# Scaling x by V's bound, turning it by halves of heads, and a new order of issue in a kernel of bucketed attention and a gated MoE

## The chip, the cores and the metric

One core of one Trainium2 chip runs the whole program. The metric is the device time of one execution in microseconds (us); lower is better. Engines are named as the profile names them: PE (TensorE, matmuls; PEld is its weight loads), DVE (VectorE), ACT (ScalarE), POOL (GpSimd), SP (SyncE, which issues the DMAs).

## What is computed

```python
# B, H, S, D = 4, 8, 768, 64; six hash bits; 3072 tokens, d_model 512, d_ff 1536
q_bits = einsum('bhsd,dk->bhsk', q, proj) > 0      # k_bits likewise
mask   = q_bucket[:, :, :, None] == k_bucket[:, :, None, :]
scores = where(mask, q @ k.T / sqrt(D), -1e9);  scores -= max(scores)
attn   = exp(scores);  attn /= sum(attn) + 1e-9
x      = (attn @ v).transpose(0, 2, 1, 3).reshape(B * S, H * D)
out    = ((x @ w_a) * (x @ w_b)) @ w_out
```

All inputs and the output are f32.

## The kernel before

**Precision.** PE works on f16. An f32 operand is scaled by a power of two and split into a high and a low f16 half, and a product is three matmuls (high by high, high by low, low by high). So each operand needs a scale: the largest magnitude per partition, `mx`, is turned by a small matmul (`ps_k`, `ps_v`, `ps_w`, L460 and L590), reduced (`al`, L466), and made into a power of two by three or four tiny DVE instructions (`scale_of`, L472 to L480; `w_scale`, L596 to L605).

**Attention.** The work is cut by batch (4), chunk of 256 tokens (3 a batch) and half of the heads (2): 24 units. `kprep` and `qprep` split K and Q (`split`, L883 on ACT or L887 on DVE for the high half, L904 for the low one), and turn them with token and feature axes exchanged (`turn`: for the first pair of K heads and the first Q by PE, `t_k` and `t_q`, with the copies L863 and L865; for all others by a DMA transpose, L844). `buckets` multiplies by proj's two halves (L816), adds the two columns of each hash bit on DVE (L825) and marks the operand with plus or minus a large number for each bit (L829), so that tokens of unequal buckets get a score far below all others. `vprep` scales V per pair of heads (`vsc`, four `ps_v` a batch; `veps`, L780) and splits it (`vh` L790, `vl` L802). `qtile` makes the scores `s` (L1053), their maximum `mx` on DVE (L1067), `width` and `bias` (L1076, L1083, L1089; `qsig` of `widths`, L995), the exponentials `e` on ACT (L1099), two f16 parts `a` (casts L1110 to L1112, low parts L1122 on POOL or L1126 on DVE), a DMA transpose `at` (L1132) and the product `av` (L1141). The first two units work in f32 with transposes `et`/`ec` by PE (`by_pe`, L1020 to L1034).

**End of a unit.** `su_end` (L1149) makes `r` (guarded sum, L1166 or L1171, and reciprocal L1179) and `x` = `av` times `r` (L1184), then the sums of |x| per token (L1195). When both halves of a chunk are there, `norm` makes a power of two per token (L1210 to L1219: 4 tiny DVE instructions for each of 2 token tiles), x is scaled by it and split (`xz`, L1237 and L1248), and each token tile is turned by one DMA transpose into `xT` (L1260). In the first and the last chunk PE turns x instead (`px`, L1283), after POOL has scaled it (L1269), and ACT and DVE write the two halves (L1295, L1298).

**MoE.** For each chunk `moe` runs twelve groups `f`: 24 matmuls `ab` (L1346), an ACT pass `a` (L1360), the product `g` on DVE (L1368), its high half (L1376 or L1380) and low half (POOL, L1388), six matmuls `o` (L1398). At the end `osc` undoes the scales per token (L1417) and `ob` is evicted (L1428, L1434, L1443) and stored (L1452). Weights are loaded (L529) and split in the first batch, beside the attention of that batch (`load_group`, `w_group`, `wo_group`, L564 to L658).

**Order.** Every operation is entered in a plan with an engine and a cost, and then issued in the order of a searched list `ORDER` (L104). A number names an operation; one above 10000 takes its first alternative engine, above 20000 its second; a negative number issues that many matmuls `warm` (L1502), which multiply an identity and are read by nobody:

```python
            if x < 0:
                fill(-x)
                continue
            which, at = divmod(x, 10000)
            o = self.ops[at]
            (o.alt[which - 1][2] if which else o.fn)()
```

Each engine then runs its own instructions strictly in that order.

Of the kernel before, what the change touches and what calls it, by code (L numbers as in the profile page):

```python
# [1540 lines left out]
```

## Time and profile before

| | |
|---|---|
| three runs | 891.77, 890.8, 888.18 us; median 890.8 |
| the profiled execution | own time 892.62 us, span 890.8 us |
| busy share of the span | PE 97%, DVE 73%, ACT 61%, POOL 48% |
| instructions | PE 9258 matmuls, DVE 1575, ACT 1043, POOL 373 |
| granted TensorE clock, mean | 0.996 of full speed |

Share of the span is an average over stages that differ. Reading starts with windows of time (which engine is full where), then goes to the chain of waits within the window that matters, and then to single groups of instructions.

### The profile page before, as it was taken

The page shows a single profiled execution, that of the slowest core. Times are in us where ns is not written, and L with a number is a line of the kernel's source. Part 1 is how long each engine was busy: PE and PEld are TensorE (multiplying, and loading weights), DVE is VectorE, ACT ScalarE, POOL GpSimd, SP SyncE. Part 2 cuts the span into 40 slices and gives each one's busy share as a digit, 9 for nine tenths or more (in the row PEclk, how much of TensorE's full clock was granted, in tenths as well). Part 3 has the DMA queues.
Part 4 walks back from the last instruction along what each step waited for, and adds up shares of the span by engine and source line. Part 5 has one row for each costly group of instructions (what it writes and reads, how often), then busy time and mean ns, then how long its engine had stood idle before and what let it go on. Part 6 is the DMA issues. An engine that isn't in the chain of part 4 may idle for free.

```text
span 890.8 us, 23135 instructions
## 1 busy us (share of the span) xinstructions
PE 866.6 (97%) x9258; PEld 661.0 (74%) x9258; DVE 650.1 (73%) x1575; ACT 542.6 (61%) x1043; POOL 425.0 (48%) x373
## 2 busy tenths in 40 slices
PE   6899999999999999999999999999999999999998
PEld 5678777777777777777777777777777777777775
DVE  6998999988877778878865676786888866663211
ACT  6998899976565685665644367536766555442212
POOL 2568788656345464563332455443455254342111
PEclk9998999999999999999999999999999999999999
DMA  9877799999999989998957598997999876645000
GB/s 325 314 157 225 133 259 190 191 188 191 169 193 204 162 145 182 199 182 176 191 103 135 84 194 142 174 201 140 174 172 168 142 139 113 117 87 92 1 24 25
DMA packets 416988, 142.61 MB, mean 160 GB/s; under 512 B 388592, under 2 KB 409200, under 8 KB 416880
## 3 DMA queue, kind: packets, MB, share of 16 engines
q1 hardware_dynamic: 416880, 141.14, 81.2%
q8 instruction: 72, 1.18, 0.5%
q14 instruction: 36, 0.29, 0.1%
HBM read 37.82 MB, written 6.29 MB: 50 GB/s over the span
## 4 chain that ended last, share of the span: by engine, by line
PE 82%; DVE 7%; DMA 6%; ACT 1%; issue 1%; POOL 1%; SPq 0%; ACTq 0%; DVEq 0%; POOLq 0%
PE ab L1346 39%; PE o L1398 20%; PE s L1053 12%; PE av L1141 9%; DMA at<-a 3%; DVE mx L1067 2%; DMA qTA_q<-marked 1%; DMA rk_k<-in_k_dram 1%; DVE wmx L634 1%; DMA raw_w<-in_moe_w_b_dram 1%; DVE wab L573 1%; PE av L1034 1%; POOL a L1122 1%; PE b_k L816 0%; DVE vl L802 0%
## 5 line engine op out<-in xcount | busy, mean ns | idle before, releaser
L1346 PE MATMUL ab<-xT,wab 128*128 128x256 f16 x3456 | 408.8, 273 | 0.9 <-DVE g L1368 0.9
L1346 PEld LDWEIGHTS <-wab 128*128 128x128 f16 x3456 | 332.8, 98 | 59.3 <-issue 2.4
L1388 POOL TENSOR_TENSOR g<-g,g 128x256 f16<-128x256 f32 x144 | 109.3, 759 | 291.0 <-ACT g L1376 155.7
L1122 POOL TENSOR_TENSOR a<-e,a 128x768 f16<-128x768 f32 x121 | 205.6, 1705 | 85.0 <-ACT a L1111 38.7
L1099 ACT ACTIVATE e<-s,bias,width 128x768 f32<-128x768 f32 x192 | 189.5, 987 | 56.7 <-DVE bias L1089 42.2
L1398 PE MATMUL o<-wo,g 128*128 128x512 f16 x864 | 207.6, 379 | 0.7 <-DVE ob L1434 0.7
L1067 DVE TENSOR_REDUCE mx<-s 128x1 f32<-128x768 f32 x192 | 182.0, 949 | 33.3 <-PE s L1053 32.4
L1368 DVE SCALAR_TENSOR_TENSOR g<-ab,wlow,a 128x256 f32<-128x256 f32 x132 | 63.6, 482 | 136.5 <-ACT a L1360 120.7
L1360 ACT ACTIVATE a<-ab,wcut 128x256 f32<-128x256 f32 x144 | 67.8, 471 | 151.1 <-PE ab L1346 149.3
L1398 PEld LDWEIGHTS <-g 128*128 128x128 f16 x864 | 81.8, 98 | 78.5 <-issue 0.8
L1141 PEld LDWEIGHTS <-at 128*128 128x128 f16 x3168 | 111.3, 98 | 18.0 <-DMA at<-a 4.6
L1141 PE MATMUL av<-vh,at 128*128 128x64 f16 x2112 | 114.8, 193 | 2.4 <-DMA at<-a 2.2
L1053 PE MATMUL s<-kTA_k,qTA_q 128*128 128x384 f16 x384 | 94.6, 328 | 3.7 <-ACT e L1099 1.8
L1053 PE MATMUL s<-kTB_k,qTB_q 128*128 128x384 f16 x384 | 94.2, 327 | 0.0
L1111 ACT CAST a<-e 128x768 f16<-128x768 f32 x85 | 70.3, 828 | 5.5 <-DMA at<-a 2.7
L1083 ACT ACTIVATE bias<-mx,width 128x1 f32<-128x1 f32 x98 | 28.6, 293 | 70.8 <-DVE width L1076 70.6
L1126 DVE TENSOR_TENSOR a<-e,a 128x768 f16<-128x768 f32 x55 | 57.5, 1049 | 8.2 <-ACT a L1111 6.0
L1112 POOL CAST a<-e 128x768 f16<-128x768 f32 x48 | 40.2, 838 | 43.4 <-ACT e L1099 23.2
L1141 PE MATMUL av<-vl,at 128*128 128x64 f16 x1056 | 59.7, 193 | 0.0
L1053 PEld LDWEIGHTS <-qTB_q 128*128 128x128 f16 x384 | 37.7, 98 | 25.3 <-issue 0.7
L1376 ACT CAST g<-g 128x256 f16<-128x256 f32 x78 | 31.2, 400 | 30.9 <-DVE g L1368 25.3
L1053 PEld LDWEIGHTS <-qTA_q 128*128 128x128 f16 x384 | 33.9, 100 | 18.6 <-issue 5.5
(156 smaller groups left out, 877.6 us busy)
## 6 DMA issues: line engine op xcount, KB each, us to landing
rk_k<-in_k_dram SPq DMA_DIRECT2D x16, 384.0 KB, 4.2
vr<-in_v_dram SPq DMA_DIRECT2D x16, 384.0 KB, 4.1
rq_q<-in_q_dram SPq DMA_DIRECT2D x12, 512.0 KB, 4.8
raw_w<-in_moe_w_b_dram SPq DMA_DIRECT2D x12, 512.0 KB, 7.4
raw_w<-in_moe_w_a_dram SPq DMA_DIRECT2D x12, 512.0 KB, 7.3
raw_wo<-in_moe_w_out_dram SPq DMA_DIRECT2D x12, 512.0 KB, 5.6
out_dram<-ob SPq DMA_DIRECT2D x24, 256.0 KB, 3.0
at<-a SPq DMA_TRANSPOSE x176, 4.1
```

What stands on the lines that cost most here:

```text
L1053: nc.tensor.matmul(ps.t[:, jj, :HALF], lhsT=x.t[:, uq, :], rhs=y.t[:, h * NT + jj * 3 : h * NT + jj * 3 + 3, :].rearrange("p t x -> p (t x)"),
L1067: lambda: nc.vector.tensor_reduce(out=mx.t[:, u : u + 1], in_=halves(ps.t), axis=AX.XY, op=ALU.max, negate=True),
L1099: lambda: nc.scalar.activation(flat2(e.t), halves(ps.t), AF.Exp, bias=bias.t[:, u : u + 1], scale=width.t[:, u : u + 1], accum_out=sm.t[:, ...
L1111: ("ACT", 0.725, lambda: nc.scalar.copy(out=a2.t[:, 0], in_=e.t), False),
L1122: lambda: nc.gpsimd.tensor_tensor(out=a2.t[:, 1], in0=e.t, in1=a2.t[:, 0], op=ALU.subtract),
L1126: lambda: nc.vector.tensor_tensor(out=a2.t[:, 1], in0=e.t, in1=a2.t[:, 0], op=ALU.subtract), True,
L1141: nc.tensor.matmul(av.t[:, u, :], lhsT=at.t[:, a + kt, :], rhs=w.t[:, h, kt, :], start=i == 0, stop=i == 3 * NT - 1,)
L1346: nc.tensor.matmul(pl.t[:, m, :CH], lhsT=wt(m, wi, cc, f), rhs=xt.t[:, :, xi * NC + cc, :], start=i == 0, stop=i == 3 * NC - 1,)
L1360: lambda a=a, pl=pl, gr=gr: nc.scalar.activation(a.t, pl.t[:, 0, :CH], AF.Copy, scale=wcut[:, gr : gr + 1]),
L1368: lambda a=a, g32=g32, pl=pl, cut=cut: nc.vector.scalar_tensor_tensor(out=g32.t, in0=pl.t[:, 1, :CH], scalar=cut, in1=a.t, op0=ALU.mult, o ...
L1388: lambda g=g, g32=g32: nc.gpsimd.tensor_tensor(out=g[1].t, in0=g32.t, in1=g[0].t, op=ALU.subtract),
L1398: nc.tensor.matmul(po.t[:, u, :], lhsT=g[gi].t[:, us], rhs=wo[f // 2].t[:, f % 2, wi * DM : (wi + 1) * DM], start=f % per_q == 0 and i == ...
```

## The change

- x is no longer normalised per token. `x_scale` makes one factor per batch from V's scales (`xinv`, `xrel`), which enters through `r`; the sums of |x|, `norm` and POOL's scaling of x are gone; `osc` is one number per chunk. In the first two units `r` is made on DVE, elsewhere on ACT or DVE.
- x is turned by halves of heads: each unit writes its own `z` (high half by ACT, DVE or POOL, low half by DVE or POOL) and issues one DMA transpose of 8 blocks, as many in all as before; in the first and last chunk one `px` of 4 blocks per unit.
- In the first batch V has one scale (`vscale_all`): four magnitudes, one `ps_v`. That matmul stands on PE right ahead of the first `t_q`, and all four V loads stand ahead of the first weights. `vh` and `vl` share a tile `vv`; `veps` is gone.
- The two columns of each hash bit are summed by PE (two accumulating matmuls) for K of the first batch and for the first Q: 64 tiny matmuls more, 5 reductions on DVE fewer.
- `widths` is one instruction in place of two (24 in place of 48 in all); the weights' `wcut` and `wone` are made for two groups at once.
- The very last `o` is issued per token tile, and the last `ob` is evicted in two halves, by ACT and by DVE.
- POOL is a new alternative for the high halves of K, Q and V. The list uses it 6, 7 and 9 times; ACT makes 4 high halves of K (before 11), 3 of Q (11) and 6 of V (14).
- `ORDER` is new. It has 112 `warm` matmuls in place of 192. In both lists all of them stand ahead of the first `ab`; ahead of the 17th score tile stood 160 of 192 and now stand 111 of 112. In all ACT has 725 instructions in place of 821, DVE 1416 in place of 1577, POOL 402 in place of 378.

```diff
-                out=sums.t[:, :, half], in_=x.t.rearrange("p (j t h) d -> p t j (h d)", j=2, t=TPC), axis=AX.XY,
-                op=ALU.add, apply_absolute_value=True,
...
-        op("DVE", 1.32, norm, key, r=[(sums, 0), (sums, 1)], w=[sc, sq])
...
+        def guarded_whole():
+            nc.vector.tensor_scalar(
+                out=r.t, in0=sm.t, scalar1=1e-9, scalar2=xinv[:, 0, 1:2], op0=ALU.add, op1=ALU.mult
+            )
...
+            z = buf("z", [P, 2, 2 * TPC, P], F16, f"z_{n}", 1)
...
+                lambda: nc.sync.dma_start_transpose(
+                    out=xt.t[:, half].rearrange("p i u x -> p (i u) x"), in_=z.t.rearrange("p i u x -> p (i u x)")
+                ),
+                key, r=[(z, "hi"), (z, "lo")], w=[(xt, half)], svc=2.2 * 8 / 12,
...
+    def vscale_all(keys, tag):
+        mx = buf("sc_mx4", [P, NPAIR + 1], F32, "mx_v", 1)
+        for hp in range(NPAIR):
+            magnitude(
+                v32[0, hp], vjunk(0, hp), lambda hp=hp: mx.t[:, hp + 1 : hp + 2], keys[hp], [(mx, hp), (vv[0, hp], "lo")]
+            )
+        op(
+            "DVE", 0.13,
+            lambda: nc.vector.tensor_reduce(out=mx.t[:, 0:1], in_=mx.t[:, 1:], axis=AX.X, op=ALU.max),
+            keys[-1], r=[(mx, hp) for hp in range(NPAIR)], w=[mx],
+        )
+        scale_of(mx, vsc[:, 0:1], xinv[:, 0, 1:2], ("v1", 0), "v", keys[-1], tag=tag)
...
             for u in range(n):
+                if summed:
+                    for i in range(2):
+                        nc.tensor.matmul(
+                            ps.t[:, 1, u * NBITS : (u + 1) * NBITS], lhsT=tB.t[:, u, :], rhs=pw[:, :, i],
+                            start=i == 0, stop=i == 1,
+                        )
+                    continue
...
+            ), (
+                "POOL", 0.1 + 0.065 * n,
+                lambda: nc.gpsimd.tensor_scalar(
+                    out=part(B, hi_at), in0=x, scalar1=sc.t, scalar2=1.0, op0=ALU.mult, op1=ALU.mult
+                ),
+                False,
...
+            for us_ in [[u] for u in range(TPC)] if alone and f == NF - 1 else [range(TPC)]:
...
+                if alone and u == TPC - 1:
+                    hs = [slice(0, DM // 2), slice(DM // 2, DM)]
...
-    6, 5, 7, 13, 4, 2, 1, 0, 53, 41, 61, 281, 277, 276, 10014, 8, 280, 9, 3, 258, 10, 15, -10, 11, 254, 257, 16,
+    4, 5, 6, 7, 13, 0, 41, 2, 1, 53, 56, 54, 55, 266, 14, 265, 3, 261, 15, -9, 262, 16, 240, 17, 42, 239, 10018, 243,
```

**ACT, ahead of the first scores.** Of before, and then of the change, from the copy of `kTA` on; `nB_k_1,mx_k_1` is the magnitude of the second K load, `qTA` the first Q that the first scores need, `raw_w` weights. The line numbers are those of each file.

```order
L863 COPY kTA_k_0_321<-t_k_0_ACT 128x1536
L550 ACTIVATE raw_w_0_125<-raw_w_0_125,wsc_335 128x1024
L550 ACTIVATE raw_w_1_123<-raw_w_1_123,wsc_335 128x1024
L751 ACTIVATE nB_k_1_400,mx_k_1_401<-rk_k_1_81 128x12x64
L863 COPY qTA_q_0_408<-t_q_0_ACT 128x2048
L790 ACTIVATE vh_0_164<-vr_0_118,vsc 128x768
```

```order
L928 COPY kTA_k_0_323<-t_k_0_ACT 128x1536
L557 ACTIVATE raw_w_0_134<-raw_w_0_134 128x1024
L549 ACTIVATE raw_w_1_128<-raw_w_1_128,wsc_373 128x1024
L549 ACTIVATE raw_w_0_134<-raw_w_0_134,wsc_373 128x1024
L928 COPY qTA_q_0_411<-t_q_0_ACT 128x2048
L758 ACTIVATE nB_k_1_421,mx_k_1_422<-rk_k_1_82 128x12x64
```

The magnitude of K's second load stood ahead of the copy of `qTA` and now stands behind it; one more pass over weights stands ahead.

**SP, ahead of the second Q's transpose.** Of before and of the change; `qTA_q_1` is the marked Q of the second chunk, `raw_w` and `rq` are loads of 0.5 MB.

```order
L844 DMA_TRANSPOSE qTB_q_1_935<-nB_q_1_741 128x16x128
L734 DMA vr_3_957<-in_v_dram 128x2x384
L529 DMA raw_w_0_973<-in_moe_w_b_dram 128x1024 x2
L529 DMA raw_w_1_986<-in_moe_w_a_dram 128x1024
L949 DMA rq_q_0_89<-in_q_dram 128x8x128
L529 DMA raw_w_1_1013<-in_moe_w_b_dram 128x1024
L529 DMA raw_w_0_1024<-in_moe_w_a_dram 128x1024 x2
L529 DMA raw_w_1_1013<-in_moe_w_b_dram 128x1024
L844 DMA_TRANSPOSE qTA_q_1_1065<-marked 128x16x128
```

```order
L909 DMA_TRANSPOSE qTB_q_1_880<-nB_q_1_789 128x16x128
L909 DMA_TRANSPOSE kTA_k_3_928<-marked 128x12x128
L1022 DMA rq_q_2_87<-in_q_dram 128x8x128
L528 DMA raw_w_1_951<-in_moe_w_b_dram 128x1024
L528 DMA raw_w_0_849<-in_moe_w_b_dram 128x1024
L1022 DMA rq_q_0_90<-in_q_dram 128x8x128
L528 DMA raw_w_1_1022<-in_moe_w_a_dram 128x1024
L528 DMA raw_w_1_951<-in_moe_w_b_dram 128x1024
L909 DMA_TRANSPOSE qTA_q_1_1040<-marked 128x16x128
```

Nine loads stood between the last transpose and this one; now six stand there.

**POOL, first third of the first batch.** Of before and of the change; `marked` is the operand that gets the bits' marks, `vv` V's halves, `wab` weights.

```order
L895 COPY marked<-nB_k_0_128 128x12x64
L564 TENSOR_SCALAR raw_w_1_123<-raw_w_1_123 128x1024
L564 TENSOR_SCALAR raw_w_0_159<-raw_w_0_159 128x1024
L895 COPY marked<-nB_k_1_400 128x12x64
L564 TENSOR_SCALAR raw_w_1_137<-raw_w_1_137 128x1024
L564 TENSOR_SCALAR raw_w_1_411<-raw_w_1_411 128x1024
```

```order
L958 TENSOR_SCALAR nB_q_0_158<-rq_q_0_83,qsc_q_0_223 128x16x64
L563 TENSOR_SCALAR raw_w_1_128<-raw_w_1_128 128x1024
L830 TENSOR_SCALAR vv_3_187<-vr_3_122,vsc 128x12x64
L966 COPY marked<-nB_q_0_158 128x16x64
L830 TENSOR_SCALAR vv_1_225<-vr_1_124,vsc 128x12x64
L830 TENSOR_SCALAR vv_0_179<-vr_0_120,vsc 128x12x64
L563 TENSOR_SCALAR raw_w_0_151<-raw_w_0_151 128x1024
L563 TENSOR_SCALAR raw_w_1_164<-raw_w_1_164 128x1024
L958 TENSOR_SCALAR nB_k_1_421<-rk_k_1_82,ks_k_1_451 128x12x64
L830 TENSOR_SCALAR vv_2_232<-vr_2_126,vsc 128x12x64
```

The high halves of the first Q, of V and of two K pairs, which ACT made, are now among POOL's instructions.

## Rows read from the trace of the kernel before

**Rows 1.** The page: busy us by engine; granted clock, tenths, in 40 slices.

```profile
PE 866.6 (97%) x9258; PEld 661.0 (74%) x9258; DVE 650.1 (73%) x1575; ACT 542.6 (61%) x1043; POOL 425.0 (48%) x373
...
PEclk9998999999999999999999999999999999999999
```

**Rows 2.** Windows: length; busy PE, PEld, DVE, ACT, POOL; clock, DMA share, GB/s.

```profile
0.00:25.00 25.00, 16.12 (x163) 12.32 (x164) 16.83 (x50) 17.88 (x21) 5.39 (x13) 1.00 0.92 334
25.00:110.00 85.00, 78.01 (x713) 64.20 (x712) 78.18 (x200) 76.44 (x127) 61.23 (x42) 0.96 0.80 201
110.00:150.00 40.00, 37.95 (x433) 28.32 (x431) 37.61 (x91) 37.80 (x61) 31.96 (x22) 1.00 1.13 238
80.00:90.00 10.00, 8.58 (x44) 7.16 (x43) 6.04 (x14) 5.61 (x10) 5.86 (x4) 0.66 0.15 48
150.00:300.00 150.00, 148.82 (x1702) 113.19 (x1701) 125.47 (x323) 102.64 (x201) 83.16 (x71) 1.00 1.01 184
```

**Rows 3.** PE by line: the filling matmuls, and the bits of K.

```profile
L1502 PE MATMUL warm<-ident 128*128 128x256 f16 x192 | 27.6, 289 | 0.0
...
L816 PE MATMUL b_k<-pjk,kTB_k 128*128 128x12 f16 x192 | 7.2, 168 | 0.3 <-DVE kTA_k L865 0.3
```

**Rows 4.** Chain of waits, 20 to 110 us: shares; start us, us, what.

```profile
by line: DVE mx L1067 14.7%; DMA qTA_q<-marked 13.7%; DMA rk_k<-in_k_dram 12.0%; DVE wmx L634 7.9%; DVE wab L573 6.4%; issue 5.7%; PE av L1034 5.6%; POOL a L1122 5.3%; DMA at<-a 4.3%; PE s L1053 4.2%; PE et L1020 2.8%; DVE wo_y L573 2.5%; P
...
21.97 0.94 ACT nB_k L751 x2
...
22.91 1.76 ACT qTA_q L863
...
69.30 12.36 DMA qTA_q<-marked
```

**Rows 5.** PE timeline around 82 us: start us, us, what [idle].

```profile
78.83 1.45 PE L1034 MATMUL av<-vr,ec 128*128 128x64 f32 x12
...
81.70 0.50 PE L1053 MATMUL s<-kTA_k,qTA_q 128*128 128x384 f16 x2 [1.42 <-DMA qTA_q<-marked]
...
83.53 2.66 PE L1034 MATMUL av<-vr,ec 128*128 128x64 f32 x12
```

**Rows 6.** DVE by line, 0 to 150 us: xcount | busy, mean ns.

```profile
L1195 DVE TENSOR_REDUCE sums<-x 128x2 f32<-128x512 f32 x2 | 1.3, 670 | 0.0
...
L825 DVE TENSOR_REDUCE b_k<-b_k 128x72 f32<-128x144 f32 x4 | 1.2, 308 | 0.0
...
L995 DVE TENSOR_SCALAR qsig_q<-kinv,qmx_q 128x1 f32<-128x1 f32 x10 | 1.6, 205 | 0.0
...
L466 DVE TENSOR_REDUCE al_v<-ps_v 128x1 f32<-128x128 f32 x4 | 1.1, 282 | 0.6 <-PE ps_v L460 0.6
...
L605 DVE TENSOR_SCALAR wcut<-wcut 128x1 int32<-128x1 int32 x6 | 0.9, 154 | 0.2
```

**Rows 7.** DVE by line, whole span: the low parts `a`.

```profile
L1126 DVE TENSOR_TENSOR a<-e,a 128x768 f16<-128x768 f32 x55 | 57.5, 1049 | 8.2 <-ACT a L1111 6.0 <-POOL a L1112 2.0
```

**Rows 8.** ACT by line, 0 to 150 us.

```profile
L1027 ACT COPY ec<-et 128x768 f32<-128x768 f32 x14 | 11.0, 789 | 0.7 <-PE et L1020 0.4
...
L650 ACT CAST wab<-wab 128x1024 f16<-128x1024 f32 x5 | 5.2, 1038 | 0.0
...
L883 ACT ACTIVATE nB_q<-rq_q,qsc_q 128x1024 f16<-128x1024 f32 x4 | 4.6, 1143 | 0.0
...
L790 ACT ACTIVATE vh<-vr,vsc 128x768 f16<-128x768 f32 x4 | 3.7, 932 | 0.0
...
L883 ACT ACTIVATE nB_k<-rk_k,ks_k 128x768 f16<-128x768 f32 x4 | 3.7, 928 | 1.2 <-DVE ks_k L480 1.2
```

**Rows 9.** Timeline of the end.

```profile
886.49 1.26 ACT L1428 ACTIVATE ob<-o,osc 128x512 f32<-128x512 f32 x2 [2.33 <-PE o L1398]
887.20 0.91 SPq L1452 DMA_DIRECT2D out_dram<-ob  x2
```

**Rows 10.** POOL by line, whole span: the casts of weights.

```profile
L653 POOL CAST wab<-wab 128x1024 f16<-128x1024 f32 x6 | 8.8, 1467 | 5.9 <-DVE wab L573 5.7
```

More of the change, by code (lines that the diff above doesn't have):

```diff
@@ L578, in to_f32, with w_scale @@
         )
-    def w_scale(g, mx, sc, cut, one, toks, name, key):
-        al = buf("sc_al", [P, 1], F32, f"al_{name}", 4)
-        pw = buf("sc_pw", [P, 1], F32, f"pw_{name}", 4)
+    def w_scale(g, mx, sc, name, key, al, m=0, more=None):
+        own = slice(m, m + 1)
         ps = psum(f"ps_{name}")
@@ L609, in rest @@
         def rest():
[L610 to L612 removed]
+            power(sc.t, 0x7F800000, -1, 143 * 8, al.t[:, own])
+        op("DVE", 0.3, rest, key, r=[(al, m)], w=[sc])
+        if more is None:
+            return
+        cut, one, toks = more
         def powers():
             if cut is None:
[L616 removed]
+                power(one, 0x7F800000, 8, 897, al.t)
             else:
[L618 to L621 removed]
+                power(cut, 0x700000, -8, 117, al.t)
+                power(one, 0x7FF00000, 8, 887, al.t)
+        op("DVE", 0.3 if cut is None else 0.62, powers, key + 2, r=[(al, x) for x in range(m + 1)], w=toks)
     def load_group(g, srcs, ats, name, key, afters=((), ())):
@@ L1061, in qtile @@
         )
-        whole = (b, c) in F32_UNITS
+        whole = (b, c, half) in F32_UNITS
         top = 0.0 if whole else LN_ESC
@@ L1266, in su_end @@
[L1266 to L1277 removed]
+        xt = xT[b, c]
@@ new lines, in flat, with side, part @@
+        def flat():
+            return x.t.rearrange("p u d -> p (u d)")
+        def side(i):
+            return xt.t[:, half, i].rearrange("p u x -> p (u x)")
+        if b * NCH + c not in X_BY_PE:
+            z = buf("z", [P, 2, 2 * TPC, P], F16, f"z_{n}", 1)
+            def part(i):
+                return z.t[:, i].rearrange("p u x -> p (u x)")
+            op(
+                "ACT", 0.51, lambda: nc.scalar.copy(out=part(0), in_=flat()), key, r=[x], w=[(z, "hi")], hold=[xt],
+                alt=[
+                    ("DVE", 0.34, lambda: nc.vector.tensor_copy(out=part(0), in_=flat()), True),
+                    ("POOL", 0.56, lambda: nc.gpsimd.tensor_copy(out=part(0), in_=flat()), False),
+                ],
+            )
+            op(
+                "DVE", 0.61,
+                lambda: nc.vector.tensor_tensor(out=part(1), in0=flat(), in1=part(0), op=ALU.subtract),
+                key, r=[x, (z, "hi")], w=[(z, "lo")], sbuf=True,
+                alt=[(
+                    "POOL", 1.1,
+                    lambda: nc.gpsimd.tensor_tensor(out=part(1), in0=flat(), in1=part(0), op=ALU.subtract), False,
+                )],
+            )
+            op(
+                "SP", T_ISSUE * 8 / 12,
+                lambda: nc.sync.dma_start_transpose(
+                    out=xt.t[:, half].rearrange("p i u x -> p (i u) x"), in_=z.t.rearrange("p i u x -> p (i u x)")
+                ),
+                key, r=[(z, "hi"), (z, "lo")], w=[(xt, half)], svc=2.2 * 8 / 12,
+            )
+            return
@@ L1278, in su_end @@
         ps = psum(f"px_{n}", tag)
         def tps():
-            for h, y in enumerate(xx):
-                for u in range(2 * TPC):
-                    nc.tensor.transpose(
-                        out=ps.t[:, h, u * P : (u + 1) * P],
-                        in_=y.t[:, 2 * u : 2 * u + 2, :].rearrange("p h d -> p (h d)"), identity=ident,
-                    )
-        def side(i):
-            return xt.t[:, :, i * NC : (i + 1) * NC, :].rearrange("p t c x -> p c t x")
-        def both():
-            return ps.t.rearrange("p h (j t x) -> p (h j) t x", j=2, t=TPC)
@@ L1294, in su_end @@
-        op("PE", 0.9, tps, key, r=[(y, "norm") for y in xx] + ["ident"], w=[ps], hold=[xt])
-        op("ACT", 0.9, lambda: nc.scalar.copy(out=side(0), in_=both()), key, r=[ps], w=[(xt, "hi")])
-        op(
-            "DVE", 1.2,
-            lambda: nc.vector.tensor_tensor(out=side(1), in0=both(), in1=side(0), op=ALU.subtract),
-            key, r=[ps, (xt, "hi")], w=[(xt, 0), (xt, 1)],
+            for u in range(2 * TPC):
+                nc.tensor.transpose(
+                    out=ps.t[:, 0, u * P : (u + 1) * P],
+                    in_=x.t[:, 2 * u : 2 * u + 2, :].rearrange("p h d -> p (h d)"), identity=ident,
+                )
@@ new lines, in su_end @@
+        op("PE", 0.45, tps, key, r=[x, "ident"], w=[ps], hold=[xt])
+        op(
+            "ACT", 0.52, lambda: nc.scalar.copy(out=side(0), in_=ps.t[:, 0]), key, r=[ps], w=[(xt, half, "hi")],
+            alt=[("DVE", 0.62, lambda: nc.vector.tensor_copy(out=side(0), in_=ps.t[:, 0]), False)],
+        )
+        op(
+            "DVE", 0.63,
+            lambda: nc.vector.tensor_tensor(out=side(1), in0=ps.t[:, 0], in1=side(0), op=ALU.subtract),
+            key, r=[ps, (xt, half, "hi")], w=[(xt, half)],
@@ L1323, in moe @@
         xt = xT[b, c]
-        xtok = [(xt, t) for t in range(TPC)]
-        sq = tsq[b, c]
+        xtok = [(xt, half) for half in range(2)]
         ob = [buf("ob", [P, DM], F32, f"ob_{b}_{c}_{u}") for u in range(TPC)]
@@ L1392, in moe, with second @@
             )
-            def second(f=f, g=g, po=po):
-                for u in range(TPC):
+            def second(us_, f=f, g=g, po=po):
+                for u in us_:
                     us = slice(u * P, (u + 1) * P)
```

375 lines of the change are left out of this document (173 added, 202 removed), and 379 rows, old and new, of the table ORDER.

## Prediction

> **What bounds the kernel now.** The page comes first [rows 1]: PE is busy 97% of the span, no other engine over 73%, and the granted clock is at its upper level, 2.4 GHz, nearly throughout. That says only that most of the span is PE's. The windows say where it is not [rows 2]. From 150 to 300 us PE is busy 148.82 of 150 us; there nothing that makes another engine faster is worth more than 1.2 us. The change leaves PE's large products as they are, so a gain must come from the first 150 us and from the end. From 25 to 110 us DVE is busy 78.18 and ACT 76.44 of 85 us, from 110 to 150 us 37.61 and 37.80 of 40: both are full at once. PE looks busy there too, 78.01 of 85, but part of that is work which nobody reads: the 192 filling matmuls, 27.6 us or 0.144 us each [rows 3].
>
> The chain of waits between 20 and 110 us names the engine that ends last [rows 4]. The largest share is DVE's `mx`, 14.7%, and DVE's weight work `wmx`, `wab` and `wo_y` adds 7.9 + 6.4 + 2.5 = 16.8%; no line of ACT is among the first ten. So DVE binds in the head, with ACT close behind, and PE's fillings stand where it waits. Two other waits are in that chain. The first scores wait for the copy of `qTA` at 22.91, which stood on ACT behind the magnitude of K's second load (0.94 us from 21.97) [rows 4]. And the DMA transpose of the second `qTA`, issued at 69.30, took 12.36 us behind a queue of loads [rows 4]; PE waited 1.42 us for it, and then the granted clock fell: the twelve f32 `av` that took 1.45 us at 78.83 took 2.66 us at 83.53 [rows 5]. In the window from 80 to 90 us the mean granted clock is 0.66, so some 6.8 of those 10 us were at the lower level, 1.2 GHz, half of which, 3.4 us, is lost; DVE and ACT were busy only 6.04 and 5.61 us of the ten [rows 2].
>
> **The change, part by part.** I count to one place, the first `ab` of the second chunk, behind which DVE has slack.
>
> DVE loses, ahead of that place: the sums of |x|, 2 x 0.67 = 1.34 us; the powers per token, 8 tiny instructions at 0.154 (the nearest row), 1.2; three of V's four scale chains, each a reduction (0.282) and three tiny ones (0.154), 3 x 0.744 = 2.2; four `veps`, 0.6; five sums of hash bits, 5 x 0.308 = 1.5; five of ten `qsig`, 5 x 0.205 = 1.0; three calls that make `wcut` and `wone`, 12 x 0.154 = 1.85. It gains one maximum over V's magnitudes (0.28 by the nearest reduction) and two tiny `r` (0.3). Together 9.7 - 0.6 = 9.1 us less [rows 6]. The new list also moves work that both kernels have: ahead of that place DVE gets four low parts `a` more, 4 x 1.05 = 4.2 us [rows 7], and is rid of three copies (two `ec`, one `kTA`), at 0.79 each by ACT's row, 2.4 [rows 8]. Net DVE has 9.1 - 1.8 = 7.3 us less to do before the same place.
>
> ACT gives away three high halves of Q and four of V to POOL, two of K to POOL and one to DVE: 3 x 1.143 + 4 x 0.932 + 3 x 0.928 = 9.9 us. It takes two `ec` (0.79), four casts of weights (1.04) and one copy like `qTA`'s (1.76): 7.5 [rows 4, 8]. Its net, 2.4 us, is the lower end for the head, if ACT were the one that binds; it is rid of some `r` and of `xz` as well, so the true figure is above 2.4. The upper end is 9.1, if what DVE takes over lies in its idle time. I take DVE's net, 7.3, because the chain names DVE.
>
> Fewer fillings: 80 x 0.144 = 11.5 us less on PE [rows 3]. That is no gain of its own, since they stand in PE's waiting time; it says that this waiting time must shrink by about as much, which fits a DVE that is 7 to 9 us shorter. The 64 more matmuls for hash bits cost 7.2/192 = 0.038 us each, 2.4 us [rows 3], and lie in the same waiting time; were PE full there, the head would give 2.4 us back.
>
> The first scores: the copy of `qTA` no longer stands behind the magnitude (0.94 us) that waited for K's load until 21.97 [rows 4], but one more pass over weights stands ahead of it, 1.04 us by the nearest row [rows 8]. The bounds are 1.0 us later and 1.9 us earlier (0.94 twice, the pass and as much of the wait); I take 0.94 earlier, the part that leaves the chain, since before 25 us DVE is busy only 16.83 us [rows 2] and work that comes sooner is done sooner. V's single scale stands on PE ahead of the first `t_q` and needs four V loads and four magnitudes of 0.94 us on ACT, two of each more than before; while they end before the first Q is split I cost it at nothing. Without that cover it is two magnitudes late, 1.9 us, and takes the 0.94 back twice over.
>
> x by halves: `z` has one buffer, so a unit's `z` waits for the last transpose of the unit before; 24 units share 890 us, so nothing waits. Transposes are as many as before. From 150 us on DVE and ACT have slack of 16% and 32% [rows 2]; the work that leaves them there buys nothing, at most the 1.2 us that PE idles.
>
> SP: ahead of the second `qTA`'s transpose six loads stand in place of nine. Of 12.36 us a third less is some 4 us, more than the 1.42 us by which it was late [rows 4, 5]. So this wait and the fall behind it, 1.4 + 3.4 = 4.8 us, may go. Against it, the fillings that remain stand nearly all ahead of the 17th score tile, so that PE meets its later waits bare. I book 0 for the two together, and keep 4.8 as an end of the range.
>
> The end: after the last `o` two evictions, 1.26 us, run in a row on ACT, and the second store follows [rows 9]. Now the first runs beside the last matmuls, and the second is shared by two engines. A half costs between 0.32 us (half of 0.63) and 0.63; I take 0.4, so 0.85 us leaves.
>
> The sum: 7.3 + 0.94 + 0.85 = 9.1 us off the profiled execution's own time of 892.62 us: 883.5. That execution stands 1.8 us above the median of the three runs (890.8), so the median becomes 881.7; I say **881.5**. With the ends of the terms (head 2.4 to 9.1, first scores -1.0 to 1.9, clock 0 to 4.8, end 0.6 to 0.95) this case reaches from 888.8 to 874.0, and most of it lies between 875 and 886.
>
> **The rivals.** *POOL shuts out DVE, and the gain is eaten: no change.* Nine high halves more stand on POOL in the head, by ACT's rows 3 x 1.143 + 4 x 0.932 + 2 x 0.928 = 9.0 us. POOL's cast of a weight tile takes 1467 ns on average, ACT's of the same size 1038 [rows 8, 10], so POOL is slowed at times; DVE's low parts average 1.05 us and do not show waits as long as a POOL operation [rows 7]. If each of the nine held DVE for its whole length, 0.1 us would remain of the gain: 890.7. The Trainium skill ("SBUF — State Buffer", section Who interferes with whom) speaks for this rival: a DVE operation with two SBUF inputs and a GpSimd operation that reads SBUF shut each other out for a whole instruction, while ACT never waits, so that moving splits from ACT to POOL would be a bad trade. The trace has the slowed POOL casts, but no DVE row longer by a whole POOL operation. Chance 0.10.
>
> *ACT binds, or the transposes do.* DVE shorter by 7 us lets PE ask for `at` earlier, and from 110 to 150 us the DMA share is already 1.13 [rows 2]. Then ACT's 2.4 us, the first scores and the end remain, 4.2 us: 886.6. Chance 0.10, half of it on either side of the line to no change.
>
> *The clock falls: slower.* With 80 fewer fillings PE waits bare between the 17th score tile and the first `ab`. For it: one wait of 1.42 us was followed by some 6.8 us at the lower level [rows 2, 5]. Against it: with less DVE work the waits are shorter, and no other slice of the page shows the clock under 9 tenths [rows 1]. A microsecond at 1.2 GHz loses half a microsecond of work, so it takes 2 x (9.1 + 4.5) = 27 us at the lower level, beyond the 6.8 of now, to be slower by over 0.5%; with 30 us the time is 881.7 + 15 = 896.7. Chance 0.08.
>
> *The fall at 82 us goes as well:* 881.7 - 4.8 = 876.9, on the forecast's side. Chance 0.22.
>
> **How the numbers follow.** 0.5%, 4.45 us, is about what a measurement of this kernel can tell from no change: faster is below 886.35, slower above 895.25. The forecast has 0.50, the case without the fall 0.22, half of the ACT or transpose case 0.05: 0.77 faster. Its other half and POOL's case: 0.15 within. The clock: 0.08 slower. The range holds the forecast's own case, the case without the fall with some of its lower end, and of no change all but the last: 872.5 to 890.
>
> **What would show it.** Right: the first `ab` about 8 us earlier; DVE and ACT still over 90% busy between 25 and 100 us and PE full from 140 us on; a granted clock of 1.00 or one short fall in the head; under 0.5 us of eviction after the last `o`. The step on DVE is wrong if the first `ab` comes earlier by under 4 us while DVE's idle time in the head grows; POOL's rival is right if DVE's low halves of K, Q and V lengthen by a whole POOL operation; the clock's, if more than two slices of the page show it under 9 tenths.

## The result, and the profile after

The changed kernel takes 901.22 us (median of four runs, 899.76 to 902.14) against 890.96 for the kernel before beside it: ratio 1.0118, interval 1.0099 to 1.0137. It is slower by 1.2%, where a gain of 1% was forecast. The profiled execution shown here took 901.29 us, its span is 899.2.

The page and the windows of the changed kernel, in the columns of [rows 1, 2]:

```profile
PE 860.0 (96%) x9239; PEld 654.1 (73%) x9239; DVE 646.4 (72%) x1414; ACT 493.0 (55%) x945; POOL 443.2 (49%) x397
...
PEclk9999899999999999999999999999999999999999
```

```profile
0.00:25.00 25.00, 14.41 (x175) 10.96 (x176) 16.99 (x46) 16.02 (x19) 10.63 (x17) 1.00 0.87 305
25.00:110.00 85.00, 73.12 (x690) 59.32 (x690) 81.37 (x175) 74.40 (x123) 57.37 (x37) 0.96 0.80 216
110.00:150.00 40.00, 37.19 (x436) 27.80 (x434) 38.62 (x77) 36.36 (x59) 31.07 (x22) 1.00 1.05 213
90.00:105.00 15.00, 12.02 (x101) 9.14 (x100) 13.23 (x25) 10.26 (x18) 9.86 (x6) 0.77 0.69 137
150.00:300.00 150.00, 145.55 (x1637) 109.34 (x1636) 128.54 (x289) 93.76 (x182) 83.89 (x73) 1.00 0.99 183
```

DVE has 161 instructions fewer in the whole program, but its busy time fell by only 3.7 us (650.1 to 646.4), and between 25 and 110 us it ran 25 instructions fewer than before and was busy longer, 81.37 against 78.18 us [rows 2]. So its instructions became longer on average there, 465 ns against 391; part of that can be another mix of instructions. Which ones took longer than before, the groups by line say (DVE, whole span; count, busy us, mean ns):

```profile
L1067 DVE TENSOR_SCALAR qsig_q<-kinv,qmx_q 128x2 f32<-128x2 f32 x24 | 12.1, 503 | 0.0
...
L1248 DVE TENSOR_SCALAR r<-sm,xrel 128x4 f32<-128x4 f32 x22 | 8.0, 405 | 1.5 <-ACT e L1169 1.5
L1253 DVE TENSOR_SCALAR r<-sm,xinv 128x8 f32<-128x8 f32 x2 | 3.8, 1904 | 0.0
L1248 DVE TENSOR_SCALAR r<-sm 128x8 f32<-128x8 f32 x2 | 1.8, 894 | 0.0
```

Before, 48 `qsig` of one column took 203 ns each on average; now 24 of two columns take 503 ns, 12.1 us in place of 7.7 for the same numbers. The timelines of DVE and of POOL, ahead of PE's longest wait between 25 and 110 us (start us, us, what), show what they do meanwhile:

```profile
89.76 1.71 DVE L1253 TENSOR_SCALAR r<-sm,xinv 128x8 f32<-128x8 f32 x1
91.39 2.17 DVE L1067 TENSOR_SCALAR qsig_q<-kinv,qmx_q 128x2 f32<-128x2 f32 x1
93.47 0.94 DVE L1137 TENSOR_REDUCE mx<-s 128x1 f32<-128x768 f32 x1
```

```profile
89.79 1.65 POOL L1192 TENSOR_TENSOR a<-e,a 128x768 f16<-128x768 f32 x1
91.41 2.12 POOL L662 TENSOR_TENSOR wab<-wab 128x1024 f16<-128x1024 f32 x1
```

`r` ends at 91.47 and POOL's `a` at 91.44; `qsig` ends at 93.56 and POOL's `wab` at 93.53. An instruction on eight or two numbers per partition lasts until 30 ns after the POOL instruction that runs beside it. Over the run 10 of 24 `qsig` lose 6.8 us in this way, 8 of 26 `r` 7.8 us, and the two-column `wcut` and `wone` and the four-column `xrel` 3.3 us more, some 18 us in all, 8.3 of them ahead of 150 us. The single column is the control: of the 618 TENSOR_SCALAR over one column in the kernel before, 327 began while a POOL instruction was running, and none was held; in the changed kernel it is none of 222 among 424, and 23 of the 68 over two to eight f32 or int32 columns.

What followed on ACT and PE:

```profile
94.69 0.29 ACT L1153 ACTIVATE bias<-mx,width 128x1 f32<-128x1 f32 x1 [2.95 <-DVE width L1146]
```

```profile
96.15 0.80 PE L1123 MATMUL s<-kTA_k,qTA_q 128*128 128x384 f16 x2 [2.81 <-ACT e L1169]
```

The 3.5 us on DVE make `mx`, `width`, `bias` and `e` late in turn; PE waits 2.81 us from 93.3 us on, and from 95.1 to 102.0 us its clock is at the lower level, 1.2 GHz: 0.77 of full over the window from 90 to 105. The wait at 82 us that this replaces [rows 5] is gone, and the transpose that caused it, issued at 69.3 us again, lands after 4.2 us in place of 12.4.

Both are single executions. The mean granted clock was 0.991 to 0.995 in the four executions of the changed kernel, and 0.995 to 1.000 (mean 0.9986) in the 65 executions of the kernel before that were taken beside the experiments. The profiled one of before, at 0.996, is thus one of its lower ones.

The end (timeline, the last 7 us):

```profile
892.40 0.69 ACT L1471 ACTIVATE ob<-o,osc 128x512 f32<-128x512 f32 x1 [2.27 <-PE o L1427]
893.12 3.48 SPq L1495 DMA_DIRECT2D out_dram<-ob  x3
895.24 0.47 ACT L1456 ACTIVATE ob<-o,osc 128x256 f32<-128x256 f32 x1 [2.15 <-DMA out_dram<-ob]
895.75 0.48 DVE L1463 TENSOR_SCALAR ob<-o,osc 128x256 f32<-128x256 f32 x1 [6.11 <-ACT ob L1456]
```

The last `o` ends at 892.37 and the span 6.8 us later; before it was 886.45 and 4.35. The first eviction still starts behind the last matmul and not beside it, the second waits 2.15 us for a store, and its two halves run one after the other. The list had put a store of the chunk before behind the last chunk's first store, and the second eviction needs its buffer.

Where the difference of the two profiled executions stands, from the timelines of PE (us):

| | first scores | first `ab` | first `ab` of chunk 2 | last `o` ends | span |
|---|---|---|---|---|---|
| before | 24.77 | 108.8 | 177.7 | 886.45 | 890.8 |
| changed | 24.93 | 102.4 | 181.5 | 892.37 | 899.2 |
| changed, run e6_all below | 24.81 | 96.4 | 172.6 | 883.74 | 888.9 |

### The profile page after: what moved, and what is told of

Read it like the earlier page. It is cut to its first block, busy times and chain, and to the rows that moved or that the text cites. A ratio compares the mean times of both kernels' runs of the same rounds, so it can differ in the third digit from the quotient of the medians.

```text
span 899.2 us, 22901 instructions
## 1 busy us (share of the span) xinstructions
PE 860.0 (96%) x9239; PEld 654.1 (73%) x9239; DVE 646.4 (72%) x1414; ACT 493.0 (55%) x945; POOL 443.2 (49%) x397
## 4 chain that ended last, share of the span: by engine, by line
PE 76%; DVE 14%; DMA 5%; issue 2%; ACT 1%; SPq 1%; POOL 0%; DVEq 0%; ACTq 0%; POOLq 0%
PE ab L1374 38%; PE o L1427 18%; PE s L1123 10%; PE av L1211 9%; DVE mx L1137 4%; DVE wmx L635 1%; DMA at<-a 1%; DVE g L1397 1%; DMA raw_w<-in_moe_w_b_dram 1%; DVE wab L572 1%; DMA raw_w<-in_moe_w_a_dram 1%; DMA raw_wo<-in_moe_w_out_dram 1%; DVE width L1146 1%; DVE wo_y L572 1%; DMA rq_q<-in_q_dram 1%
## 5 line engine op out<-in xcount | busy, mean ns | idle before, releaser
L1192 POOL TENSOR_TENSOR a<-e,a 128x768 f16<-128x768 f32 x114 | 190.3, 1674 | 90.9 <-ACT a L1181 40.3
L1211 PEld LDWEIGHTS <-at 128*128 128x128 f16 x3168 | 113.3, 99 | 17.1 <-DMA at<-a 1.1
L1211 PE MATMUL av<-vv,at 128*128 128x64 f16 x3168 | 118.4, 194 | 0.9 <-DMA at<-a 0.9
L1196 DVE TENSOR_TENSOR a<-e,a 128x768 f16<-128x768 f32 x62 | 62.4, 1008 | 8.2 <-ACT a L1181 5.5
L1181 ACT CAST a<-e 128x768 f16<-128x768 f32 x76 | 62.5, 827 | 1.6 <-DMA at<-a 0.9
L1153 ACT ACTIVATE bias<-mx,width 128x1 f32<-128x1 f32 x88 | 25.4, 292 | 64.8 <-DVE width L1146 64.3
L1405 ACT CAST g<-g 128x256 f16<-128x256 f32 x70 | 28.1, 402 | 35.1 <-DVE g L1397 26.9
L1146 DVE TENSOR_SCALAR width<-mx,qsig_q 128x1 f32<-128x1 f32 x192 | 39.9, 210 | 4.3
```

Source lines behind the costliest of these rows:

```text
L1181: ("ACT", 0.725, lambda: nc.scalar.copy(out=a2.t[:, 0], in_=e.t), False),
L1192: lambda: nc.gpsimd.tensor_tensor(out=a2.t[:, 1], in0=e.t, in1=a2.t[:, 0], op=ALU.subtract),
L1196: lambda: nc.vector.tensor_tensor(out=a2.t[:, 1], in0=e.t, in1=a2.t[:, 0], op=ALU.subtract), True,
L1211: nc.tensor.matmul(av.t[:, u, :], lhsT=at.t[:, a + kt, :], rhs=w.t[:, h, kt, x, :], start=i == 0, stop=i == 3 * NT - 1,)
```

## The experiments

Theory A: a DVE TENSOR_SCALAR over two or more columns shares something with POOL that one over a single column doesn't need, and is shut out for whole POOL instructions. Theory B: POOL's 22 additional splits take DVE's time, as the rival in the prediction had it. Theory C: the new list is worse in itself. In the first group the kernel before took 889.77 us. Differences from the changed kernel are differences of medians from different groups. By the ratios, each to the kernel before of its own group, the changed kernel stands 10.5 us above it, e1_narrow 4.0, e2_store 9.1, e7_qsig 7.8, e8_r 6.4 and e9_fill 8.2; the differences given below are thus sure to about 1 us.

**e1_narrow.** `qsig` one column at a time, and every `r` on ACT (`guarded` is the function that issues it there):

```diff
-            lambda: nc.vector.tensor_scalar(
-                out=sig.t[:, 2 * half : 2 * half + 2], in0=kinv[:, at : at + 2], scalar1=mx.t,
+            lambda: [
+                nc.vector.tensor_scalar(
+                    out=sig.t[:, 2 * half + x : 2 * half + x + 1], in0=kinv[:, at + x : at + x + 1], scalar1=mx.t,
+                    scalar2=SCALE, op0=ALU.mult, op1=ALU.mult,
+                )
+                for x in range(2)
+            ],
...
-            for js, y, z in parts():
-                nc.vector.tensor_scalar(
-                    out=r.t[:, js], in0=sm.t[:, js], scalar1=y, scalar2=z, op0=ALU.mult, op1=ALU.add
-                )
+            guarded()
...
-            nc.vector.tensor_scalar(
-                out=r.t, in0=sm.t, scalar1=1e-9, scalar2=xinv[:, 0, 1:2], op0=ALU.add, op1=ALU.mult
+            nc.vector.tensor_scalar(out=xeps, in0=xinv[:, 0, 1:2], scalar1=1e-9, scalar2=None, op0=ALU.mult)
+            nc.scalar.activation(r.t, sm.t, AF.Identity, scale=xinv[:, 0, 1:2], bias=xeps)
```

> The changed kernel, with `qsig` again as two instructions on one column each, and `r` always made by ACT (in the first two units with one tiny DVE instruction more for its bias). Theory A: a DVE TENSOR_SCALAR over two or more f32 columns in SBUF cannot start its work while a POOL instruction runs, and ends some 20 to 30 ns after it; in the trace `qsig` loses 6.8 us so, and `r` 7.8 us, of that 6.8 us before 145 us, and the fall of the clock at 95 us (3.4 us) follows one such pair. Then the time falls from 901.2 to 887 to 894 us and no `qsig` is longer than 0.25 us. Theory B (POOL's additional splits of K, Q and V take DVE's time) and theory C (the new list itself is worse, whatever these instructions do): 899 to 902 us.

Measured: 894.19 us, 7.0 less than the changed kernel, with 24 instructions more on DVE for `qsig`. The group of `qsig` (DVE, whole span) is where it was before the change:

```profile
L1069 DVE TENSOR_SCALAR qsig_q<-kinv,qmx_q 128x1 f32<-128x1 f32 x48 | 7.8, 204 | 0.0
```

That is 0.2 us above the range of A, and far from B and C. Two things besides the shape changed: every `r` left DVE altogether, and the mean granted clock of the executions rose from 0.993 to 0.996.

**e2_store.** One entry of the list, the store 3340, moved ahead of 3342:

```diff
-    3528, 3342,
+    3528, 3340, 3342,
...
-    3598, 3340, 3599,
+    3598, 3599,
```

> The changed kernel, with one entry of the list moved: the store of the last chunk but one's first tile is issued ahead of that chunk's other store, and no longer behind the last chunk's first store. In the trace the last eviction waits 2.15 us for that store, since it uses its buffer. Theory A and B and C say the same here: 2.2 us less, 898.5 to 899.5 us. If the end is bound by the output DMA itself, no change (901).

Measured: 898.61 us, 2.6 less. In its trace the span ends 4.5 us behind the last `o` in place of 6.8, so this one store is worth 2.3 us there, most of what the end lost.

**e3_splits_act.** All 22 high halves of K, Q and V that POOL makes go back to ACT, by 22 entries of the list like the first:

```diff
-    12, 20044, 10059,
+    12, 44, 10059,
```

> The changed kernel, with all 22 high halves of K, Q and V that POOL makes given back to ACT, in the same places of the list. Theory A: the instructions that DVE is shut out by are mostly POOL's low parts of `a` and of weights, which stay; ACT gets 9 us more work in the first batch: 899 to 905 us. Theory B: the 8 us that the forecast expected come back, 891 to 895 us.

Measured: 908.84 us, 7.6 more than the changed kernel, where theory B expected 6 to 10 less. The loss is larger than A expected. From 25 to 110 us ACT is busy 78.35 of 85 us, against 74.40 in the changed kernel, and DVE still 79.75:

```profile
25.00:110.00 85.00, 69.81 (x663) 56.61 (x662) 79.75 (x174) 78.35 (x126) 51.84 (x31) 0.99 0.77 211
```

As ACT gets more to do here, the run alone does not clear POOL's splits. The sign that the prediction named for them does: DVE's low halves of K, Q and V, of before and then of the change (DVE, whole span), take 51.7 us in all against 50.6, and not longer by a whole POOL instruction each.

```profile
L802 DVE SCALAR_TENSOR_TENSOR vl<-vr,vsc,vh 128x768 f16<-128x768 f32 x16 | 17.8, 1112 | 1.0 <-ACT vh L790 0.9
L904 DVE SCALAR_TENSOR_TENSOR nB_k<-rk_k,ks_k,nB_k 128x768 f16<-128x768 f32 x16 | 16.8, 1048 | 1.4 <-ACT nB_k L883 1.3
L904 DVE SCALAR_TENSOR_TENSOR nB_q<-rq_q,qsc_q,nB_q 128x1024 f16<-128x1024 f32 x12 | 16.0, 1335 | 0.0
```

```profile
L838 DVE SCALAR_TENSOR_TENSOR vv<-vr,vsc,vv 128x768 f16<-128x768 f32 x16 | 17.4, 1086 | 1.3 <-POOL vv L830 1.2
L974 DVE SCALAR_TENSOR_TENSOR nB_k<-rk_k,ks_k,nB_k 128x768 f16<-128x768 f32 x16 | 17.3, 1078 | 0.7 <-POOL nB_k L958 0.4 <-ACT nB_k L948 0.2
L974 DVE SCALAR_TENSOR_TENSOR nB_q<-rq_q,qsc_q,nB_q 128x1024 f16<-128x1024 f32 x12 | 17.0, 1414 | 0.1
```

And of the 23 narrow instructions that were held in the changed kernel only 2 ended behind one of POOL's splits; 9 ended behind its low parts of `a`, the others behind its work on weights, copies, casts of `a`, `g` and `z`. So theory B falls.

**e5_before_wide.** The converse, in the kernel before: `qsig` on two columns, and `r` of the first two units on DVE over eight. Nothing else is touched, and the list is the old one.

```diff
-            lambda: [
-                nc.vector.tensor_scalar(
-                    out=sig.t[:, 2 * half + x : 2 * half + x + 1], in0=kinv[:, at + x : at + x + 1], scalar1=mx.t,
+            lambda: nc.vector.tensor_scalar(
+                out=sig.t[:, 2 * half : 2 * half + 2], in0=kinv[:, at : at + 2], scalar1=mx.t,
...
-                nc.scalar.activation(r.t, sm.t, AF.Copy, scale=1.0, bias=1e-9)
+                nc.vector.tensor_scalar(
+                    out=r.t, in0=sm.t, scalar1=1.0, scalar2=1e-9, op0=ALU.mult, op1=ALU.add
```

> The kernel before, with `qsig` made by one instruction on two columns (24 in place of 48), and `r` of the first two units made by DVE on eight columns in place of ACT. DVE has 22 instructions fewer. Theory A: some of the 24 wait for whole POOL instructions of 0.8 to 2.1 us, in the full first 110 us above all: slower, 892 to 897 us, with `qsig` of up to 2 us in the trace. Theory B and C: 890 to 891 us, or up to 1 us faster.

Measured: 897.03 us against 889.77, ratio 1.0090 (1.0059 to 1.0121): 7.3 us slower for 22 instructions fewer, at the upper end of A's range (892 to 897). The two groups (DVE, whole span):

```profile
L994 DVE TENSOR_SCALAR qsig_q<-kinv,qmx_q 128x2 f32<-128x2 f32 x24 | 12.1, 510 | 0.0
L1163 DVE TENSOR_SCALAR r<-sm 128x8 f32<-128x8 f32 x2 | 1.5, 750 | 0.0
```

So merging tiny instructions, counted as a saving in the forecast, costs 7.3 us here, and it does so without the new list (C) and without POOL's splits (B). In its trace all 14 of the 26 wide instructions that began while a POOL instruction was running were held, and none of 296 over one column.

**e7_qsig and e8_r**, the two halves of e1_narrow apart (the first and the second part of its diff), and **e9_fill**, which puts 22 fillings ahead of the scores that waited, in a second group (889.64 us before):

```diff
-    1056, 589,
+    1056, -22, 589,
```

> The changed kernel with `qsig` alone made one column at a time. Of 6.8 us that it loses in the trace of the change 2.1 lie ahead of 110 us, where DVE is full, and one of them stands in the wait ahead of the fall of the clock. Theory A: 2 to 5 us less, 896 to 899 us.

> The changed kernel with `r` alone moved to ACT. Of 7.8 us that it loses 4.8 lie ahead of 145 us. Theory A: 3 to 6 us less, 895 to 898 us; together with the run before about the 7.0 us of the first run.

Measured: 898.50 and 896.94 us, 2.7 and 4.3 less than the changed kernel; their sum is the 7.0 of e1_narrow, closer than the spread of the runs warrants (e7_qsig took 894.54 to 899.97 us). e8_r takes the work off DVE as well as its wait, so its 4.3 us are not the price of the wait alone.

> The changed kernel with 22 filling matmuls (2.4 us of PE) ahead of the scores that waited 2.81 us at 96 us, after which the granted clock fell to 1.2 GHz for 6.8 us. If the fall follows the bare wait and costs 3.4 us: no fall there, 897.5 to 899.5 us. If the wait for DVE is all that matters there (PE catches up anyway): 900 to 902 us.

Measured: 897.98 us, 3.2 less. PE's timeline has the fillings where the wait was, and the window from 90 to 105 us the upper level of the clock throughout:

```profile
93.25 2.56 PE L1557 MATMUL warm<-ident 128*128 128x256 f16 x22
96.23 0.48 PE L1126 MATMUL s<-kTA_k,qTA_q 128*128 128x384 f16 x2 [0.41 <-ACT e L1172]
```

```profile
90.00:105.00 15.00, 13.57 (x142) 10.61 (x141) 14.48 (x31) 11.60 (x20) 10.82 (x7) 1.00 0.83 139
```

The scores start at 96.23 in place of 96.15, so in the profiled execution the wait is as long as it was, and what came back is the clock. Over the four executions the mean granted clock rose from 0.993 to 0.997, an estimated 3.6 us of 899, which agrees; but one of the four, at 0.994, was no slower (898.07 us).

**e6_all.** The edits of e1_narrow and e2_store, `wcut`, `wone` and `xrel` on one column too, and DVE evicting the whole second tile of the last chunk, beside ACT's whole first (`xrel` is cut like `wcut`, by head pairs):

```diff
-                power(cut, 0x700000, -8, 117, al.t)
-                power(one, 0x7FF00000, 8, 887, al.t)
+                    power(cut[:, at], 0x700000, -8, 117, al.t[:, at])
+                    power(one[:, at], 0x7FF00000, 8, 887, al.t[:, at])
...
-                        lambda u=u, osc=osc, po=po, h=hs[0]: nc.scalar.activation(
-                            ob[u].t[:, h], po.t[:, u, h], AF.Copy, scale=osc.t
-                        ),
+                        lambda: None,
...
-                            out=ob[u].t[:, h], in0=po.t[:, u, h], scalar1=osc.t, scalar2=None, op0=ALU.mult
+                            out=ob[u].t, in0=po.t[:, u, :], scalar1=osc.t, scalar2=None, op0=ALU.mult
```

> The changed kernel with three mendings at once: no DVE instruction on two or more f32 or int32 columns is left among the tiny ones (`qsig`, `wcut`, `wone`, `xrel` one column each, `r` on ACT), the store is moved as in the second run, and at the very end DVE evicts the whole second tile while ACT evicts the first, in place of two halves that ran one after the other. From the first two runs: 901.2 - 7.0 - 2.6 = 891.6; the end gives about 0.8 more (in the second run's trace the second half ended 1.61 us after the last `o`, two whole tiles side by side take 0.75), and the last narrow ones about 1. Theory A: 888.5 to 891.5 us, no difference from the kernel before that can be told. If the parts overlap in the same waiting time: 892 to 895.

Measured: 891.71 us (12 runs), ratio to the kernel before 1.0024 (1.0013 to 1.0035): just above A's range, and still some 2 us slower than before. The eviction beside ACT gained nothing: DVE began at 884.50, 30 ns behind ACT's end, as it still carries a wait for it. The windows of e6_all:

```profile
25.00:110.00 85.00, 76.55 (x761) 62.31 (x760) 81.67 (x195) 80.47 (x136) 61.91 (x40) 1.00 0.90 234
...
150.00:300.00 150.00, 146.77 (x1667) 111.00 (x1665) 125.75 (x291) 93.19 (x188) 84.01 (x76) 1.00 0.98 181
```

In this trace the second chunk starts 5.1 us earlier than before (table above), of 8.2 that the forecast had for that place. Part of the 5.1 is the clock: this execution has no fall in the head (mean clock 0.999), and the profiled one of before has 6.8 us of it, worth up to 3.4. But from 150 to 300 us PE is busy 146.77 us against 148.82 [rows 2], and the last `o` ends only 2.7 us earlier.

**e10_act_end and e11_moves**, in a third group (890.09 us before). The first is e6_all with the second eviction on ACT, as before had it (the diff is against the changed kernel):

```diff
-                            ob[u].t[:, h], po.t[:, u, h], AF.Copy, scale=osc.t
+                            ob[u].t, po.t[:, u, :], AF.Copy, scale=osc.t
...
-                        lambda u=u, osc=osc, po=po, h=hs[1]: nc.vector.tensor_scalar(
-                            out=ob[u].t[:, h], in0=po.t[:, u, h], scalar1=osc.t, scalar2=None, op0=ALU.mult
-                        ),
+                        lambda: None,
```

> The changed kernel with narrow tiny instructions and the moved store, as in the sixth run, but with the end of the kernel before: ACT evicts both last tiles whole, one after the other. In the sixth run's trace DVE's eviction began only when ACT's had ended (it carries a wait for it), 1.51 us from the last `o` to the last eviction's end; in the kernel before it was 1.30 and the span ended 4.35 us after the last `o`, against 5.16 there. Expected: 0.2 to 0.8 us less than the sixth run's 891.7, 890.9 to 891.5 us.

Measured: 891.08 us, ratio 1.0011 (0.9999 to 1.0022): not to be told from the kernel before.

The second moves three pieces of DVE's weight work (`w_end`, twice `wo_y`) in e10_act_end's list, away from POOL's work beside them:

```diff
-    648, 678,
+    648, 371, 678,
...
-    681, 371, 675,
+    681, 675,
...
-    491, 833,
+    491, 419, 833,
...
-    11084, 419, 826,
+    11084, 826,
...
-    892, 443, 880,
+    892, 880,
...
-    526, 1062,
+    526, 443, 1062,
```

> The kernel of the run before with three entries of the list moved, and nothing else: the DVE instruction `w_end` and the two `wo_y` that took 2.66 to 2.68 us in the sixth run's trace in place of 1.22, because POOL's low part of `a` had begun just ahead of them, are issued a few DVE instructions earlier (two) or behind the next `g` (one). Theory A extended to two-input instructions: 3 to 4 us of DVE's time come back between 120 and 170 us, PE's waits for `g` at 147 and 168 us (0.99 and 1.16 us) go, and the time falls by 1 to 3 us, to 888 to 890.5. If what the head gained is given back for another reason (DMA, PE itself): no change from the run before.

Measured: 891.11 us, no change, where 1 to 3 us were expected. The shutouts that it aimed at are gone (groups of DVE between 110 and 180 us; in e10_act_end the mean of the four `wo_y` is 1948 ns and `w_end` takes 2686):

```profile
L576 DVE SCALAR_TENSOR_TENSOR wo_y<-raw_wo 128x1024 int32<-128x1024 int32 x4 | 4.9, 1230 | 0.0
L576 DVE SCALAR_TENSOR_TENSOR w_end<-raw_w 128x1024 int32<-128x1024 int32 x1 | 1.5, 1484 | 0.0
```

and so are most of PE's waits for `g`, 3.4 us in e10_act_end and 0.9 now; but a `wab`, an `a` and a `vv` of DVE, behind them in its order, now take 2.18, 2.39 and 2.43 us, and PE waits 1.5 us ahead of a `ps_k`, and 2.3 in place of 1.1 for `e`.

**e12_more_fill.** e10_act_end with 40 fillings more ahead of early waits (a negative entry is a number of fillings):

```diff
-    21, -14, 43,
+    21, -23, 43,
...
-    23, -4, 267,
+    23, -9, 267,
...
-    25, -9, 72,
+    25, -20, 72,
...
-    49, -4, 271,
+    49, -9, 271,
...
-    74, -15, 156,
+    74, -25, 156,
```

> The tenth run's kernel with 41 more filling matmuls at five places between 12 and 31 us where PE waits bare (waits of 0.5 to 1.3 us in its trace): 9, 5, 11, 5 and 10 (and one by rounding of the places, 40 to 41 in all). In its trace the granted clock fell at 21.3 us for 3.4 us, and over the twelve executions the mean granted clock (0.996 to 0.999) and the time (892.9 to 889.4) go together. If the fall follows the bare waits: fewer falls, a mean clock of 0.998 to 1.000, 889 to 890.5 us. If fillings only delay what stands behind them: 891 to 893.

Measured: 892.88 us, ratio 1.0033 (1.0022 to 1.0044), 1.8 more than without them. A miss: the mean clock of the executions was 0.997 to 1.000, hardly better than the 0.996 to 0.999 of e10_act_end, and the fillings cost more than they gave.

## Why the prediction was wrong

**The reading of what binds was right in the main.** In the changed kernel's chain of waits from 20 to 110 us DVE's `mx` again has the largest share, 17.6%, and the held instructions stand in the chain themselves:

```profile
66.26 2.02 DVE r L1253
...
89.84 1.63 DVE r L1253
91.47 2.08 DVE qsig_q L1067
```

What DVE waits costs time: 22 instructions fewer on it, but some 8.5 us of waiting more, made the kernel before 7.3 us slower (e5_before_wide). Only some 3 of the 8.5 lie ahead of 150 us, though, so DVE's waits behind the head are not free either. And ACT is as close as the prediction said: 22 passes more on it cost 7.6 us (e3_splits_act).

**The step that failed is the count of DVE's time: "Net DVE has 9.1 - 1.8 = 7.3 us less to do before the same place."** It priced `qsig`, `r`, `wcut` and `wone` by the rows of instructions on one column, 0.15 to 0.21 us [rows 6], and the change makes them two or eight columns wide there; and four such `r`, not two, stand on DVE ahead of 150 us. Ahead of 150 us these instructions lost 8.3 us to POOL, more than the 7.3 counted. The trace of before could not show it of `qsig`, as it has 48 of one column and not one that waits; the step should have said that the shape had changed, and bounded the price from above by a POOL instruction, some 2 us. The sign that the prediction set for this step did not catch it: the first `ab` came 6.4 us earlier, and only that of the second chunk, the place it had counted to, came 3.8 us later.

**The rival about POOL had the right rule and the wrong carrier.** It let the nine additional POOL splits hold DVE, at a chance of 0.10 and for no change. What matters is which DVE instructions can be held: DVE's low halves took hardly longer, giving the splits back made it worse (e3_splits_act), narrowing DVE's tiny instructions mended most of it (e1_narrow). The means of its rows also hid what the trace of before had: one `wab` of DVE, at 116.49 us, took 2.67 us where others take 1.22, beside a POOL `a` from 116.20 to 118.08. The Trainium skill ("SBUF — State Buffer", section Who interferes with whom) says both things: that a DVE instruction with two SBUF inputs is shut out, which the rival used, and that `tensor_scalar` can enter a mode with two ports and is shut out then, which it overlooked. The trace agrees with the second: 10 of 24 `qsig` on two columns end 20 to 30 ns behind a POOL instruction, none of 48 on one column does. The Trainium skill ("VectorE: DVE Perf Modes", section Mode 2×_2P) has that mode for f32 operands in SBUF whose outermost dimension beyond one is even, or odd and equal in source and destination. That two columns use that mode, no run shows directly, but the waits are as it would have them.

**The end, booked at 0.85 us saved, cost 2.5.** The first eviction did not start beside the last matmuls, the halves ran in a row, and a store stood late on SP. The last is worth 2.3 us by its trace and 2.6 by the medians (e2_store). The prediction looked at SP for the second Q and not for the end.

**The clock, booked at 0, was right for the two profiled executions only.** There the fall at 82 us went, as the six loads in place of nine suggested, and one of the same length came at 95 us in a wait that the shutouts made; filling that wait gave back 3.2 us (e9_fill). Over all executions the term was too small: with a mean granted clock of 0.9932 against 0.9986 the changed kernel lost an estimated 4.8 us more of its 899 to the lower level, if PE had work all that time. That is close to half of the 10.3 us by which it is slower. What brought on the falls in the executions that were not profiled is not shown. The slower rival asked for 27 us or more at the lower level; by the lowest mean, 0.991, it was at most 16.

**What lies behind the place.** The prediction said of DVE and ACT from 150 us on that "the work that leaves them there buys nothing, at most the 1.2 us that PE idles". From 150 to 300 us PE idles 4.45 us (145.55 of 150) against 1.2 before, but 3.4 of them lie ahead of the second chunk's first `ab` at 181.5 us and belong to the head; from there to 300 us PE idles 1.1 us, as before. From that `ab` to the end of the last `o`, however, the changed kernel takes 710.9 us and e6_all 711.1 against 708.7 before (table above), so some 2 us are given back where nothing was booked. Shutouts of two-input DVE instructions are seen in e6_all, but taking three of them away by hand moved them elsewhere (e11_moves). Whether another list would keep the head's lead is open.

**The first scores did not come earlier** (24.93 us): the copy of `qTA` was free of the magnitude, but the transposes ahead of it, which wait for DVE's marks, ran at 21.78 us in place of 20.28. V's single scale, costed at nothing, did cost nothing there: the first `t_q` starts at 13.71 us, and at 13.66 before.

Of the gap of 19.7 us between forecast and measurement, the tiny instructions account for 7.0, the store for 2.6, and the end's missed saving for at most 0.85; the clock's share lies within these and the rest, not beside them. The other 9 are the second chunk's start, 3.1 us short of the forecast even in e6_all, what is given back behind it, and parts that no run took alone.

## What to carry to other kernels

Fewer instructions are not less time: before two tiny TENSOR_SCALAR of DVE on one f32 column each are merged into one of two columns, look whether POOL is busy beside them, since the merged one may wait for a whole POOL instruction. A mean over a group hides such a wait, so look at the longest of a group as well. Compare the granted clock of several executions, and not of the profiled one alone. When a change alters the shape of an instruction, its row in the old trace is no longer its price. And when an end is made finer, look at the waits that its instructions carry and at the queue of stores, or the pieces run one after the other.

## What was not expected of the hardware

A TENSOR_SCALAR of DVE over 2, 4 or 8 f32 columns took up to 2.17 us beside POOL, and one over a single column at most 0.27 us through the whole run, beside the same POOL instructions. The op matters too: the 24 RECIPROCAL of `r` over 8 f32 columns took at most 0.20 us each, and 11 of them began while a POOL instruction was running. In a bare PE wait of 2.81 us the clock fell to its lower level for 6.8 us, worth 3.2 us, and with 22 fillings in the wait (to 95.81 of 96.23 us) it did not fall; 40 fillings spread over shorter waits at 12 to 31 us did not pay.
